# A gated mix of full and windowed attention: first key weights by ACT's queue, last keys and last norm in halves, a third slice for GpSimd, and a new order

## The chip, the core and the metric

The kernel runs on one core of a Trainium2 chip. The metric is the device time of one execution in microseconds. Before the change it is 780.96 us, the median of three runs (780.86 to 782.89). The traces come from one profiled execution each. Engines go by the names of the profile: PE (TensorE, matmuls), PEld (its weight loads), DVE (VectorE), ACT (ScalarE), POOL (GpSimd) and SP (which issues most transfers). L12 is line 12 of the kernel.

## The reference

The input x is one sequence of 2048 tokens and 640 features in bf16. Two attentions with 32 heads of 20 features are computed from it, one over all keys, one over a dilated window of 8 keys, and their outputs are mixed by a gate.

```
B, S, D = 1, 2048, 640
g = sigmoid((x * gate_w).sum(-1, keepdims=True))
# A: full attention
q, k, v = split_heads(x @ A_wqkv)              # 32 heads of 20
p = softmax(q @ k.T * 20 ** -0.5)
a = merge_heads(p @ v) @ A_wo
# B: token s sees s, s-2, ..., s-14, with weights of its own
b = merge_heads(softmax_over_8(q . k[s - 2 w]) . v[s - 2 w]) @ B_wo
out = g * a + (1 - g) * b
```

## The kernel before, in words

**Units and tiles.** The scores of A are computed as keys by queries. Work is cut into groups (512 queries, four heads; 32 groups) and, within a group, into units of one head, 128 keys and 512 queries: 64 per group, 2048 in all. A tile is two or three units: PE writes their scores into PSUM (L1941, `qk`), and ACT takes the exponential of a whole tile into `ebuf` (L1959, `exp`). The sums over keys, weighted by v, go to one PSUM bank, `obank` (L2004, `pv`). Four heads stand on top of each other, so four units go through PE side by side.

**Units without ACT.** Some units take another way. DVE shifts and clamps the raw score into a 16-bit integer (`clamp`, L1918, tile `uD`), which read as bf16 is a coarse exponential. Three copies of it, each with another constant added (`SHIFTS`), are made as tile `eD`, and PE adds the four slices, weighted by constants in copies of v (`vS`, L1087 on POOL), in `obank`. Such units are taken in quads: the four heads of one block of keys. In the text a slice is one of these copies, k = 1, 2, 3. `gen_d` (L1037) makes what is left of a slice with one DVE instruction of 512, 1024, 1536 or 2048 columns. `piece` lets POOL make one unit of a slice ahead of it (L1068); it looks at the slices in `KPIECE`, (1, 2) before. `eD` has room for three slices, and a slice's room is free when the one three before it has gone through PE.

**The order.** The file holds its own scheduler: `_Sched.task` books each operation on an engine with an assumed duration and derives the semaphores from the buffers that it reads and writes. Generators (`gen_b` and `gen_bproj` for attention B, `gen_norm`, `gen_fold`, `gen_v`, `gen_q1` and others) offer side work, which is put between the tiles. When an operation is taken, and whether a tile carries a quad's unit, hangs on some twenty constants (`SLACK`, `DWAIT`, `DIDLE`, `PTAPS`, ...). `PLAN` replaces them at given tile numbers: 126 sets before. All of this runs when the program is built; on the chip each engine has a fixed list, which it works off in order. POOL's operations are booked into windows beside DVE instructions of at least 0.59 us that don't use the port that DVE and POOL share, as the code has it (`slot`). `PTAPS` says how many products of attention B are made by POOL (L1196, L1304).

**The start.** SP loads x in eight pieces of 256 tokens (`x_load`, L553), the key weights of the first four heads behind the first piece (L558), and later the query weights (L561) and the rest. POOL pads the weights (L653). PE transposes x piece by piece (`turn`, L1633), ACT and DVE copy the result to `xT` (L1643, L1647), and PE computes the keys of the first four heads in four blocks of 512 (`k_first`, L1653). For each block DVE finds the largest absolute key (`k_max`, L1670), and ACT copies the block to `kT` (`k_out`, L1677). From the maxima and the absolute queries (ACT L1730, DVE L1731) comes a bound per query that is subtracted from the scores: L1712, L1714, L1728, then a matmul (L1735). The order of the start is a string, `HEAD`, with a letter for the operation and a digit for the block.

**The end.** The last group's sums are normalized by `gen_norm_last`: transpose, reciprocal, gate, scale and transpose back, each over all 512 queries. `tail` adds the last four heads to the projected output. The earlier heads are added before that, in `gen_prefold`, `gen_prefold2` and the first part of `tail`. The last fold runs through the right strips of four blocks of 128 tokens (128 columns each), then the left 512 columns of blocks 2, 3, 0 and 1. DVE adds the strips to what was computed before (L1458), ACT copies blocks 2 and 3 (L1464), DVE adds blocks 0 and 1 (L1467), and four transfers write them out (L1472).

**The output weights of B.** `constants` loads them (L644, tile `woBp`), in four transfers, each when SP's queue is quiet.

Of the kernel before, what the change touches and what calls it, by code (L numbers as in the profile page):

```python
# [5 lines left out]
FP32 = mybir.dt.float32  # L6
# [46 lines left out]
    0: ((0.326, 0.478), 0.0, 1, 1.0, 0.79, -1.09, -0.25, 10.72, 2.0, 9.17, 0.45, 0.36, 3.46, 3.61, 0.0, 0.59, 1, -2.32, 0.3, -1.0, (2, 2)),  # L53
    5: ((0.318, 0.419), 0.0, 1, 1.0, 0.79, -1.09, -0.25, 4.03, 2.0, 9.17, 0.45, 0.52, 3.46, 3.61, 0.0, 0.59, 1, -2.32, 0.3, -1.0, (2, 2)),
    10: ((0.326, 0.478), 0.16, 1, 1.79, 0.79, -1.26, -0.25, 11.51, 3.71, 8.58, 0.4, 0.67, 3.16, 3.61, -0.23, 0.59, 1, -5.33, 0.3, -1.0, (0, 2)),
    15: ((0.34, 0.55), 0.16, 1.0, 1, 0.75, -1.26, -0.13, 7.8, 4.71, 6.0, 0.91, 0.2, 6.33, 4.29, 0.03, 0.59, 1, -5.33, 0.3, -1.0, (2, 2)),
    20: ((0.34, 0.55), 0.25, 6.6, 1.0, 1.09, -1.26, -0.13, 7.8, 6.7, 7.19, 0.85, 0.32, 3.46, 4.29, 0.0, 0.71, 1, -3, 0.3, -1.0, (2, 0)),
    25: ((0.373, 0.716), 0.27, 6.6, 1.0, 1.21, -1.26, -0.13, 11.42, 6.7, 7.19, 0.85, 0.32, 3.46, 4.29, 0.0, 0.71, 1, -3, 0.3, -1.0, (2, 0)),
    30: ((0.343, 0.845), 0.31, 6.6, 1.0, 1.21, -1.26, -0.25, 11.42, 6.7, 7.19, 0.85, 0.32, 3.46, 4.29, 0.0, 0.71, 1, -3, 0.3, -1.0, (0, 2)),
    35: ((0.34, 0.55), 0.16, 1.0, 1, 0.69, -1.26, -0.43, 7.8, 4.71, 6.0, 0.91, 0.49, 5.31, 4.29, -0.03, 0.59, 1, -5.33, 0.3, -1.0, (2, 0)),  # L60
    40: ((0.326, 0.478), 0.16, 1, 1.79, 0.79, -1.26, -0.25, 11.51, 3.71, 8.58, 0.4, 0.67, 3.16, 3.61, -0.03, 0.59, 1, -5.33, 0.3, -1.0, (0, 2)),
    45: ((0.326, 0.478), 0.16, 1, 4.63, 0.79, -1.26, -0.25, 11.51, 3.71, 8.58, 0.4, 0.67, 3.16, 3.61, 0.12, 0.59, 1, -5.33, 0.3, -1.0, (1, 2)),
    50: ((0.34, 0.51), 0.25, 1, 1.0, 0.89, -1.26, -0.43, 7.8, 8, 5.03, 0.91, 0.32, 5.31, 3.77, 0.08, 0.59, 2, -6, 0.3, -1.0, (2, 2)),
    55: ((0.34, 0.51), 0.33, 1, 1.0, 0.89, -1.26, -0.24, 11.51, 8, 9.17, 0.65, 0.32, 5.31, 4.74, 0.08, 0.59, 2, -6.71, 0.3, -1.0, (2, 2)),
    60: ((0.353, 0.546), 0.33, 1, 1.0, 0.89, -1.26, -0.24, 11.51, 8, 9.17, 0.65, 0.32, 5.31, 4.74, 0.08, 0.59, 2, -6.71, 0.3, -1.0, (2, 2)),
    65: ((0.34, 0.51), 0.39, 1, 1.0, 0.89, -1.26, -0.43, 7.8, 7.0, 9.43, 0.91, 0.32, 5.31, 4.07, 0.08, 0.59, 2, -6, 0.3, -1.0, (2, 2)),
    70: ((0.34, 0.51), 0.4, 1, 1.0, 0.89, -1.26, -0.43, 7.8, 7.0, 9.43, 0.91, 0.3, 5.31, 4.07, 0.08, 0.59, 2, -6, 0.3, -1.0, (2, 2)),
    75: ((0.34, 0.51), 0.4, 1, 1.0, 0.89, -1.26, -0.94, 7.8, 7.0, 9.43, 0.91, 0.3, 5.31, 4.07, 0.08, 0.59, 2, -6, 0.3, -1.0, (2, 2)),
    85: ((0.34, 0.51), 0.4, 1, 1.0, 0.75, -1.26, -0.94, 7.8, 7.0, 9.43, 0.91, 0.3, 5.31, 3.41, 0.08, 0.59, 2, -6, 0.3, -1.0, (2, 2)),
    90: ((0.34, 0.51), 0.4, 1, 1.0, 0.75, -1.26, -0.34, 7.8, 7.0, 9.43, 0.83, 0.3, 5.31, 3.41, 0.08, 0.59, 2, -6, 0.3, -1.0, (2, 0)),  # L70
    95: ((0.389, 0.582), 0.4, 1, 1.0, 0.96, -1.26, -0.34, 7.8, 7.0, 9.43, 0.83, 0.39, 5.31, 3.41, 0.08, 0.69, 2, -6, 0.3, -1.0, (2, 0)),
    100: ((0.389, 0.582), 0.4, 1.13, 1.0, 0.96, -1.26, -0.34, 7.8, 7.0, 7.05, 0.98, 0.39, 5.31, 3.41, 0.08, 0.69, 2, -6, 0.3, -1.0, (1, 0)),
    105: ((0.389, 0.582), 0.4, 1.13, 1.0, 0.96, -1.26, -0.34, 7.8, 7.0, 7.05, 0.98, 0.65, 5.31, 3.25, 0.08, 0.69, 2, -6, 0.3, -1.0, (1, 0)),
    110: ((0.34, 0.51), 0.25, 1.13, 1.0, 0.96, -1.26, -0.43, 7.8, 1, 5.03, 0.98, 0.61, 5.31, 2.74, 0.08, 0.69, 2, -6, 0.3, -1.0, (2, 2)),
    120: ((0.278, 0.663), 0.39, 1.0, 1.0, 1.17, -1.6, -1.28, 2, 1, 4.68, 0.56, 0.57, 4.56, 4.29, -0.03, 0.65, 2, -5.46, 0.3, -1.0, (2, 2)),
    125: ((0.291, 0.715), 0.39, 1.0, 1.0, 0.94, -1.6, -0.92, 2, 2.0, 4.68, 0.64, 0.57, 4.56, 4.29, 0.0, 0.68, 2, -3, 0.3, -1.0, (2, 2)),
    130: ((0.291, 0.715), 0.39, 1.0, 1.0, 0.94, -1.48, -0.92, 2, 1, 4.68, 0.64, 0.57, 4.56, 4.29, -0.05, 0.68, 2, -3, 0.3, -1.0, (2, 2)),
    135: ((0.291, 0.715), 0.39, 1.0, 1.0, 0.94, -1.48, -0.92, 2, 1, 4.68, 0.64, 0.57, 4.56, 4.29, -0.11, 0.68, 2, -3, 0.3, -1.0, (2, 2)),
    140: ((0.291, 0.715), 0.39, 1.0, 1.0, 0.94, -1.48, -0.92, 7.8, 1, 4.68, 0.64, 0.32, 4.56, 4.29, 0.0, 0.68, 2, -3, 0.3, -1.0, (2, 2)),
    145: ((0.241, 0.719), 0.39, 1.0, 1.0, 0.94, -1.48, -0.92, 7.8, 1, 4.68, 0.64, 0.32, 4.56, 4.29, 0.0, 0.68, 2, -3, 0.3, -1.0, (2, 2)),  # L80
    150: ((0.241, 0.719), 0.39, 1.0, 1.0, 0.79, -1.48, -0.92, 7.8, 1, 4.68, 0.64, 0.32, 4.56, 4.29, 0.0, 0.73, 2, -1.5, 0.3, -1.0, (2, 2)),
    155: ((0.241, 0.719), 0.41, 1.61, 1.0, 0.79, -1.48, -0.92, 9.65, 1, 4.68, 0.69, 0.32, 4.56, 4.29, 0.0, 0.73, 2, -1.5, 0.3, -1.0, (2, 2)),
    160: ((0.241, 0.719), 0.41, 1.61, 1.0, 0.79, -1.48, -0.92, 9.65, 8, 4.68, 0.69, 0.32, 4.56, 4.7, 0.0, 0.73, 2, -1.5, 0.3, -1.0, (2, 2)),
    165: ((0.241, 0.719), 0.41, 1.61, 1.0, 0.79, -1.48, -0.92, 9.65, 1, 4.89, 0.69, 0.32, 4.56, 4.7, 0.0, 0.73, 2, -1.5, 0.3, -1.0, (2, 2)),
    170: ((0.207, 0.746), 0.41, 1, 1.0, 0.79, -1.48, -0.92, 9.65, 1, 5.2, 0.69, 0.32, 4.56, 4.7, 0.0, 0.73, 2, -1.5, 0.3, -1.0, (2, 2)),
    175: ((0.207, 0.746), 0.41, 1, 1.0, 0.79, -1.75, -0.92, 9.33, 1, 5.2, 0.69, 0.32, 4.56, 4.7, 0.0, 0.73, 2, -1.5, 0.3, -1.0, (1, 0)),
    180: ((0.207, 0.746), 0.41, 1, 1.0, 0.79, -1.75, -0.92, 9.33, 1, 5.2, 0.69, 0.32, 4.56, 4.7, 0.08, 0.73, 2, -1.5, 0.3, -1.0, (1, 0)),
    185: ((0.421, 0.553), 0.41, 1, 1.0, 0.79, -1.75, -0.34, 7.8, 1, 6.0, 0.69, 0.32, 6.33, 4.7, 0.08, 0.59, 2, -1.5, 0.3, -1.0, (1, 0)),
    190: ((0.421, 0.553), 0.41, 1, 1.0, 0.79, -1.75, -0.43, 7.8, 1, 7.54, 0.96, 0.32, 6.33, 4.7, 0.08, 0.59, 2, -1.5, 0.3, -1.0, (0, 2)),
    195: ((0.421, 0.553), 0.41, 1, 1.0, 0.79, -1.75, -0.43, 4.47, 1, 7.54, 0.96, 0.32, 6.33, 4.8, 0.08, 0.59, 2, -1.5, 0.21, -1.0, (0, 2)),  # L90
    200: ((0.421, 0.553), 0.33, 1, 1.0, 0.75, -1.75, -0.43, 4.47, 1, 7.54, 0.96, 0.32, 6.33, 4.8, -0.1, 0.59, 2, -1.5, 0.21, -1.0, (0, 2)),
# [327 lines left out]
def _build(ctx, nc, A_x, A_wqkv, A_wo, B_wqkv, B_wo, gate_w, out):  # L419
# [185 lines left out]
    def constants():  # L605
# [35 lines left out]
        for j in range(4):  # L641
            while not quiet():
                yield ("cond",)
# [1594 lines left out]
```

## Time and profile before

The profiled execution took 780.83 us; its span, from the first to the last instruction, is 779.0 us, and 1.83 us lie around it. The granted TensorE clock is 1.000.

| stage | us of the span | what is busy |
|---|---|---|
| start, to the first exponential | 0 to 18.52 | transfers and warm-up matmuls, then PE, ACT and DVE in turn |
| body, exponentials | 18.52 to 769.78 | ACT 745.19 of 751.30 with the exponentials alone |
| end | 769.78 to 779.0 | norm on DVE, folds on PE, transfers out |

| operation | count | mean ns | busy us |
|---|---|---|---|
| exponential, ACT L1959 | 710 | 1197 | 745.2 |
| clamp, DVE L1918 | 428 | 681 | 287.2 |
| slices, DVE L1037, all shapes | 287 | 620 | 171.7 |
| slice pieces, POOL L1068 | 288 | 617 | 173.6 |
| weighted v, POOL L1087 | 107 | 615 | 65.9 |
| filler matmuls, PE L2025 | 324 | 379 (median) | 27.6 |

How to read such lines: a group has its line, engine and operation, the tile written and the tiles read, the shapes and the count; behind the first bar the busy time in us and the mean ns of one; behind the second the idle time of the engine just before these instructions, and what ended most of it. Mean times of instructions that overlap on their engine add up to more than the busy time. A chain has the start in us, the length in us, and what it was.

### The profile page before, as it was taken

The page shows a single profiled execution, that of the slowest core. Times are in us where ns is not written, and L with a number is a line of the kernel's source. Part 1 is how long each engine was busy: PE and PEld are TensorE (multiplying, and loading weights), DVE is VectorE, ACT ScalarE, POOL GpSimd, SP SyncE. Part 2 cuts the span into 40 slices and gives each one's busy share as a digit, 9 for nine tenths or more (in the row PEclk, how much of TensorE's full clock was granted, in tenths as well). Part 3 has the DMA queues.
Part 4 walks back from the last instruction along what each step waited for, and adds up shares of the span by engine and source line. Part 5 has one row for each costly group of instructions (what it writes and reads, how often), then busy time and mean ns, then how long its engine had stood idle before and what let it go on. Part 6 is the DMA issues. An engine that isn't in the chain of part 4 may idle for free.

```text
span 779.0 us, 30108 instructions
## 1 busy us (share of the span) xinstructions
PE 747.8 (96%) x12412; PEld 288.3 (37%) x12412; DVE 695.2 (89%) x1245; ACT 758.2 (97%) x749; POOL 333.8 (43%) x570
## 2 busy tenths in 40 slices
PE   8999999999999999999999999999999999999987
PEld 5433333232343433433344324333444433343223
DVE  6688898999899999998899999988999998799995
ACT  5999999999999999999999999999999999999995
POOL 4133553445543543333355344624444553333531
PEclk9999999999999999999999999999999999999999
DMA  7321212011121423311123233024112421320311
GB/s 230 114 62 39 52 43 61 24 42 24 44 66 45 98 55 96 93 48 35 48 70 84 57 81 94 20 52 102 45 30 60 106 53 49 89 55 22 91 44 40
DMA packets 71456, 49.89 MB, mean 64 GB/s; under 512 B 43096, under 2 KB 64872, under 8 KB 71320
## 3 DMA queue, kind: packets, MB, share of 16 engines
q1 hardware_dynamic: 71032, 47.64, 24.3%
q8 instruction: 99, 1.62, 0.9%
q14 instruction: 37, 0.30, 0.1%
q10 hardware_dynamic: 288, 0.33, 0.1%
HBM read 32.79 MB, written 7.62 MB: 52 GB/s over the span
## 4 chain that ended last, share of the span: by engine, by line
PE 49%; ACT 27%; issue 11%; DVE 11%; DMA 2%; SPq 0%; POOL 0%; DVEq 0%; ACTq 0%
ACT ebuf L1959 27%; PE score L1941 15%; PE obank L2004 14%; PE side L687 12%; PE score L687 4%; DVE uD L1918 3%; DVE eD L1037 2%; DVE kvw L1314 1%; DVE qkvB L1143 1%; DVE kvw L1205 1%; DMA woBp<-in_B_wo_dram 1%; PE side L1218 1%; DMA oTd<-in_A_x_dram 1%; PE side L1326 1%; DMA scr_q<-qbnd 0%
## 5 line engine op out<-in xcount | busy, mean ns | idle before, releaser
L1959 ACT ACTIVATE ebuf<-score 128x1024 bf16<-128x1024 f32 (+1 forms) x710 | 745.2, 1197 | 3.1 <-PE score L1941 2.0
L1918 DVE TENSOR_SCALAR uD<-score 128x512 int16<-128x512 f32 x428 | 287.2, 681 | 34.5 <-PE score L1941 32.1
L1941 PE MATMUL score<-qT,kT 32*128 32x512 bf16 x1856 | 259.0, 384 | 12.7 <-ACT ebuf L1959 9.2
L1068 POOL TENSOR_TENSOR eD<-uD,two 128x256 int32<-128x256 int32 x288 | 173.6, 617 | 116.8 <-DVE eD L1037 53.7
L1037 DVE TENSOR_SCALAR eD<-uD 128x2048 int16<-128x2048 int16 (+3 forms) x287 | 171.7, 620 | 5.7 <-PE obank L2004 5.0
L2004 PE MATMUL obank<-ebuf,vA 128*21 128x512 bf16 x1620 | 153.3, 385 | 0.3
L1941 PEld LDWEIGHTS score<-qT,kT 32*128 32x128 bf16 x1856 | 64.0, 91 | 210.4 <-ACT ebuf L1959 149.8
L1087 POOL TENSOR_TENSOR vS<-vA,vw 128x252 bf16<-128x252 bf16 x107 | 65.9, 615 | 117.2 <-DVE eD L1037 63.5
L2004 PE MATMUL obank<-eD,vS 128*21 128x512 bf16 x1284 | 110.8, 380 | 0.4 <-POOL eD L1068 0.3
L687 PE MATMUL side<-xT,wBs 128*32 128x256 bf16 x2400 | 97.4, 281 | 2.9 <-DVE qkvB L1143 1.4
L687 PEld LDWEIGHTS side<-xT,wBs 128*32 128x32 bf16 x2400 | 68.4, 141 | 33.9 <-issue 15.4
L1010 POOL TENSOR_TENSOR oN<-oTt,oN 128x256 bf16<-128x256 f32 x60 | 44.8, 746 | 74.3 <-DVE eD L1037 37.8
L2004 PEld LDWEIGHTS obank<-ebuf,vA 128*21 128x21 bf16 x1620 | 36.8, 89 | 83.6 <-issue 62.4
L995 POOL TENSOR_TENSOR rcp<-rcp,gA 128x16 f32<-128x16 f32 x30 | 7.6, 252 | 95.6 <-DVE eD L1037 63.6
L1143 DVE CAST qkvB<-side 128x512 bf16<-128x512 f32 (+1 forms) x72 | 42.1, 594 | 4.5 <-PE side L687 4.2
L1205 DVE TENSOR_TENSOR kvw<-qkvB 128x2048 bf16<-128x2048 bf16 (+2 forms) x40 | 45.0, 1146 | 0.6 <-PE side L1218 0.5
L1314 DVE TENSOR_TENSOR kvw<-kvw,eB 128x2048 bf16<-128x2048 bf16 (+1 forms) x40 | 45.5, 1157 | 0.0
L2004 PE MATMUL obank<-uD,vA 128*21 128x512 bf16 x428 | 41.5, 379 | 0.0
L2004 PEld LDWEIGHTS obank<-eD,vS 128*21 128x21 bf16 x1284 | 30.8, 91 | 20.2 <-DVE eD L1037 2.3
L687 PE MATMUL side<-xT,kvw 128*32 128x512 bf16 (+1 forms) x360 | 30.4, 383 | 0.8 <-DVE vA L913 0.2
L1941 PE MATMUL score<-woBp,kT 32*128 32x512 bf16 x192 | 30.0, 384 | 0.5
L687 PE MATMUL side<-kvw,xT 128*32 128x160 bf16 (+1 forms) x700 | 27.4, 265 | 1.3 <-DVE small L749 0.6
(195 smaller groups left out, 566.6 us busy)
## 6 DMA issues: line engine op xcount, KB each, us to landing
kvw<-scr_v SPq DMA_DIRECT2D x32, 336.5 KB
oN<-scr_n SPq DMA_DIRECT2D x60, 128.0 KB
scr_v<-qkvB SPq DMA_DIRECT2D x32, 85.0 KB
wBs<-in_B_wqkv_dram SPq DMA_DIRECT2D x5, 480.0 KB
WqP<-in_A_wqkv_dram SPq DMA_DIRECT2D x14, 160.0 KB
oTd<-oN SPq DMA_DIRECT2D x108, 20.0 KB
out_dram<-outsb SPq DMA_DIRECT2D x12, 160.0 KB
qT<-dst SPq DMA_DIRECT2D x93, 20.0 KB
```

The costliest lines, as they stand in the source:

```text
L687: ins = e.matmul(o[j:k, :], l(j) if callable(l) else l[:, j:k], r, start=(first and i == 0), stop=(last and i == n - 1), skip_group_check= ...
L1010: T("pool", 0.73, lambda e, cols=cols: e.tensor_tensor(oN[0][:, cols], oTt[:, cols], rcpR[:, cols], ALU.mult), reads=["oTt", "oN%d" % i], ...
L1037: T("dve", 0.065 + 0.1334 * (n - m), lambda e, k=k, sl=sl, m=m: e.tensor_scalar(eD[:, sl % NS, 512 * m:512 * n].bitcast(I16), uD[d % 2][:, ...
L1068: T("pool", PDUR, lambda e: e.tensor_tensor(eD[:, sl % NS, 512 * i:512 * (i + 1)].bitcast(I32), uD[d % 2][:, 512 * i:512 * (i + 1)].bitcas ...
L1087: T("pool", 0.607, lambda e: e.tensor_tensor(vS[:, d % 2, :, :], _ap(vA, (kb * NQ + q) * 4 * DV, [[0, K - 1], [1, 4 * DV]]), _ap(vw, 0, [[ ...
L1143: t = TB(dvc(n * TOK), lambda e, o=o, i=i: e.tensor_copy(o, i), reads=[("side", b)], writes=[key])
L1205: TB(dvc(n_ * TOK, 2), lambda e: e.tensor_tensor(o, i0, i1, ALU.mult), reads=["qB", "kB"], writes=prods(i, range(n_)) + olds(), port=True)
L1314: TB(dvc(n_ * 2 * TOK, 2), lambda e: e.tensor_tensor(o, i0, i1, ALU.mult), reads=rd, writes=prods(i, range(2 * n_)), port=True)
L1918: t = T("dve", 0.598, lambda e: e.tensor_scalar(uD[d % 2][:, 512 * i:512 * (i + 1)].bitcast(I16), side[x], UOFF, 0.0, op0=ALU.add, op1=ALU ...
L1941: ins = e.matmul(o, kT[32 * j:32 * j + 32, q, kb * P:(kb + 1) * P], qT[qbuf[g]][32 * j:32 * j + 32, :], start=True, stop=True)
L1959: exps[s] = T("act", actc(512 * n), lambda e: e.activation(ebuf[s % NE][:, 0:512 * n], score[s % 2][:, 0:512 * n], ACTF.Exp, scale=LN2 / S ...
L2004: ins = e.matmul(obank[32 * j:32 * j + DV, :], v, src, start=(kb == 0), stop=(last and k >= len(lst) - 4), skip_group_check=True)
```

## The change

1. The transfer of the first key weights is issued by ACT's queue instead of SP's, and the eight pieces of x follow each other on SP. The query weights stay on SP.
2. The keys of the first heads are computed in five blocks instead of four: three of 512 and two of 256. Block 2 goes to PSUM bank 2 instead of bank 0, block 3 to bank 0, block 4 to `obank`. The maximum is taken and the block copied for each of the five. The second half of the absolute queries is made by ACT instead of DVE.
3. The last norm is made in halves of 256 queries, second half first, and the last fold goes half by half: strips of blocks 2 and 3, their left columns, strips of blocks 0 and 1, their left columns.
4. `KPIECE` is (1, 2, 3): POOL may make pieces of the third slice too. `PLATE`, how late a piece may start, becomes a constant of the plan (0.13 to 0.28).
5. `woBp` may be loaded when the scheduler is past group 12, quiet or not.
6. `PLAN` has 121 sets of 22 values in place of 126 sets of 21. Only 4 of the tile numbers that occur in either keep the values that held there.
7. Some assumed durations and issue times of the scheduler differ.

The diff without the plan, cut to its core:

```diff
-    x_load(0, 4.1)
-    T("sp", 4.6, lambda e: e.dma_start(w4(ebuf[3]), wA_v[:, :, D:D + 4 * DH]), writes=[("ebuf", 3)], dma=True, iss=0.5)
-    for p, t in enumerate((5.4, 6.6, 7.4, 8.3, 9.2, 10.1, 11.0)):
-        x_load(p + 1, t - 0.78 - 0.28 * p)
+    T("act", 5.0, lambda e: e.dma_start(w4(ebuf[3]), wA_v[:, :, D:D + 4 * DH]), writes=[("ebuf", 3)], dma=True, iss=0.45)
+    for p, t in enumerate((4.0, 5.6, 6.5, 7.4, 8.3, 9.2, 10.1, 11.1)):
+        x_load(p, t - 0.28 * p)
...
-        while not done.get(("norm", 8)) or g1 <= QLAST or not done.get(("qs", 1, 2)) or not calm():
+        while not done.get(("norm", 8)) or g1 <= QLAST or not done.get(("qs", 1, 2)) or not (calm() or cur["g"] > 12):
...
-            while not quiet():
+            while not (quiet() or cur["g"] > 12):
...
-        T("dve", 0.625, lambda e: e.transpose(oTt[:, :], obank[:, :]), reads=["obank"], writes=["oTt"])
...
+        for op, h in ((turn_o, 1), (turn_o, 0), (inv, 1), (inv, 0), (gate_r, 1), (gate_r, 0), (scale_o, 1), (scale_o, 0), (back, 1), (back, 0)):
+            op(h)
...
-    KPIECE = (1, 2)
+    KPIECE = (1, 2, 3)
...
-        mm(("score", 1), [fold_mms(strip(blk), blk, q, 512, D, False)[0] for blk in range(4)], True)
-        for blk in (2, 3):
-            b = tail_bank[blk]
-            mm(("side", b), fold_mms(side[b][:, :], blk, q, 0, 512, False), True)
-        for blk in range(2):
-            mm(("score", 0), fold_mms(half(blk), blk, q, 0, 512, False), True)
+        for h in (1, 0):
+            mm(("score", 1), [fold_mms(strip(blk), blk, q, 512, D, False)[0] for blk in (2 * h, 2 * h + 1)], True, rd[h])
+            for blk in (2 * h, 2 * h + 1):
+                if h:
+                    b = tail_bank[blk]
+                    mm(("side", b), fold_mms(side[b][:, :], blk, q, 0, 512, False), True, rd[h])
+                else:
+                    mm(("score", 0), fold_mms(half(blk), blk, q, 0, 512, False), True, rd[h])
...
-    kbank = lambda tcc: ((side[0], ("side", 0)), (side[1], ("side", 1)), (side[0], ("side", 0)), (obank, "obank"))[tcc]
+    kbank = lambda i: ((side[0], ("side", 0)), (side[1], ("side", 1)), (side[2], ("side", 2)), (side[0], ("side", 0)), (obank, "obank"))[i]
+    kcol = lambda i: ((0, 512), (512, 512), (1024, 512), (1536, 256), (1792, 256))[i]
...
-    HEAD = ("t0 w0 w1 x0 t1 x1 y0 y1 a0 t2 b0 x2 y2 m0 t3 x3 o0 t4 y3 x4 y4 t5 k1 y5 x5 t6 x6 m1 t7 x7 y6 k2 o1 "
-            "y7 k3 m2 o2 q0 c0 m3")
+    HEAD = ("t0 x0 w0 w1 t1 x1 y0 y1 a0 t2 b0 x2 y2 m0 t3 x3 o0 t4 y3 x4 y4 t5 k1 y5 x5 t6 x6 m1 t7 x7 y6 k2 o1 "
+            "y7 k3 m2 k4 o2 m3 q0 c0 o3 m4")
...
-    T("dve", dvc(256), lambda e: e.tensor_scalar(
-        qabs[0][:, 256:512].bitcast(U16), side[2].bitcast(U16)[:, 1:512:2], 0x7FFF, None, op0=ALU.bitwise_and),
-      reads=[QB[1]], writes=[("qabs", 0)])
+    T("act", actc(256), lambda e: e.activation(qabs[0][:, 256:512], qb[1], ACTF.Abs), reads=[QB[1]], writes=[("qabs", 0)])
...
-             FILL, HOLD, BOFF, EVS, FRT, PTAPS) = plan
+             FILL, HOLD, BOFF, EVS, FRT, PTAPS, PLATE) = plan
```

The letters of `HEAD`: t transposes a piece, x and y copy it (ACT, DVE), a and b are the halves of the first key block, k is a key block, m its maximum, o its copy to `kT`, q the first queries, c the maximum over the earlier blocks, w a warm-up matmul.

## The prediction

> **What bounds the kernel now.** I read the page's busy shares first, then a table of busy time over the stretch in which the exponentials run, then the groups of instructions with their shapes, and last the chains at both ends, because a bound read from the whole span mixes three stages.
>
> ```profile
> PE 747.8 (96%) x12412; PEld 288.3 (37%) x12412; DVE 695.2 (89%) x1245; ACT 758.2 (97%) x749; POOL 333.8 (43%) x570
> L1959 ACT ACTIVATE ebuf<-score 128x1024 bf16<-128x1024 f32 (+1 forms) x710 | 745.2, 1197 | 3.1 <-PE score L1941 2.0
> ```
>
> These are two lines of the page. ScalarE's 710 exponentials fill 745.2 us and were kept waiting 3.1 us in all. The first starts at 18.52 us and the last ends at 769.78, by the timeline. The table by stretches, 20 to 770 us, closes with this sum:
>
> ```profile
> sum 750.00, PE 726.18 PEld 274.98 DVE 678.58 ACT 746.35 POOL 324.15; mean PE 90.77 PEld 34.37 DVE 84.82 ACT 93.29 POOL 40.52
> ```
>
> Of 750.00 us ACT is busy 746.35, so 3.65 are idle, while DVE idles 71.4 and GpSimd 425.9. PE looks nearly as full, but 324 of its matmuls, 81 groups of four, are fillers (L2025) that give way to real work. So the body, 751.3 us, is ACT's: it gets shorter only when units of work leave ACT. A unit is one head's 128 keys by 512 queries. There are 2048; DVE takes the 428 of L1918, ACT 1620, which is 745.2/1620 = 0.460 us each. DVE takes units four at a time, a "quad" (107 of them). One quad more takes 4 x 0.460 = 1.84 us from the body.
>
> What a quad costs DVE, and what GpSimd takes of that, stands in the groups by shape:
>
> ```profile
> L1918 DVE TENSOR_SCALAR uD<-score 128x512 int16<-128x512 f32 x428 | 287.2, 681 | 34.5 <-PE score L1941 32.1
> L1068 POOL TENSOR_TENSOR eD<-uD,two 128x256 int32<-128x256 int32 x288 | 173.6, 617 | 116.8 <-DVE eD L1037 53.7 <-DVE kvw L1314 18.3 <-DVE uD L1918 16.7
> L1037 DVE TENSOR_SCALAR eD<-uD 128x2048 int16<-128x2048 int16 x203 | 137.1, 692 | 5.5 <-PE obank L2004 5.0
> ...
> L1037 DVE TENSOR_SCALAR eD<-uD 128x512 int16<-128x512 int16 x20 | 5.8, 291 | 0.1
> ```
>
> A quad is four clamps of 0.681 and three shifted slices of 0.692, 4.80 us. A slice of one unit takes 0.291, of four 0.692, so one unit less saves (0.692 - 0.291)/3 = 0.134 us, and the last one 0.291. GpSimd now makes 288 pieces of one unit, of the first two slices only.
>
> The start is not ACT's. Its chain begins so:
>
> ```profile
> 0.74 0.46 SPq L553
> 1.20 0.06 issue
> 1.25 0.46 SPq L558
> 1.71 0.04 issue
> 1.75 5.01 DMA oTd<-in_A_x_dram
> 6.76 0.05 issue
> ```
>
> SP issues input piece 0, then the key weights (L558), then piece 1, whose data are there at 6.76; PE has nothing but warm-ups until then. The end is PE's. Its last pieces:
>
> ```profile
> 770.44 2.16 PE score L687 x40
> 772.60 1.53 PE score L1436 x64
> 774.13 0.22 PE side L1436 x4
> 774.35 0.68 PE score L1436 x12
> 775.03 0.02 issue
> 775.05 0.69 DVE kvw L1467
> ```
>
> PE folds without a break from the last attention matmul (770.23) to 775.03. The last norm, on DVE, runs from 770.28 to 772.76 beside it (the timeline's L943 to L952), and PE asks for it only at about 773.5. It has 0.75 us of room.
>
> **The change part by part**, against the profiled execution: 780.83 us, of which 779.0 are the span and 1.83 lie around it. The median of three is 780.96, 0.13 above.
>
> **Start, key weights by ACT's queue.** SP loses one issue, 0.50 us (1.25 to 1.75), ahead of piece 1 and the six after it. On ACT the issue comes before its table load (1.28) and warm exponential; nothing on ACT is needed until 5.08, and the warm one ends at 2.24, so 0.46 is hidden; without that cover it would cost its 0.46. GpSimd waits for these weights (L653 at 4.22); their product is asked for at 7.33, with 2.6 us of room for 0.52 of copy. Best case: the dip in DMA traffic closes too (84 to 161 GB/s between 3.5 and 5 us, over 300 after), about 1.0 us in all. Worst case: from 5 to 16 us the DMA engines are full (364 to 394 GB/s at their best), piece 5 still lands at 10.47, where PE waits 0.37 today, and the gain is 0. I take 0.5, the issue itself, nearest to a row. The Trainium skill (Trainium Kernel Development and Optimization, "Key Constraints"; DMA: Bandwidth & Descriptors, "Issuing engines are not separate DMA queues") says that DMAs from several engines run on the same 16 DMA engines and that only issue time is saved; by it the gain is these 0.5, and the 1.0 is ruled out. The trace of before has one queue here, so it can't show it.
>
> **Start, last 512 keys in halves, bound of the first queries on ACT.** One product of 1.24 us becomes two halves on PE, the same columns. On DVE the chain from 14.56 to 16.72 (maximum 0.70, small ones 0.17 and 0.29, maximum 0.68, L1728 0.35) becomes 0.70 + 0.41 + 0.46 + 0.41 + 0.35 = 2.33 instead of 2.16 (0.41: a 256-column row, L1143's 413 ns). That is 0.2 later. In exchange the 0.42 of L1731, now behind it, goes to ACT, whose copies (0.68, and half that) leave it free at about 16.8; its two absolutes of 0.38 end near 17.1, where L1731 ended at 17.15. New wait: the second query product takes bank 2, which the third key block now holds until ACT has copied it (about 16.0); PE reaches it at 16.2. Between -0.1 and +0.2; I take 0.
>
> **Body, GpSimd on the third slice and a new order.** Pieces run beside DVE's 512-column reads. The groups list 428 + 48 + 30 + 20 + 20 + 20 + 16 + 12 + 8 + 5 = 607 of these, and GpSimd work placed in them is 288 + 107 + 60 + 30 + 24 + 22 = 531. So 76 windows at most are open, worth 76 x 0.134 = 10.2 us of DVE, which pays for two quads (9.6). With DVE's own 71.4 idle us the ceiling is far higher, (71.4 + 10.2)/4.80 = 17 quads, -31 us; the floor is that no piece more is made, 0, or that a different order is worse, below. I take **two quads, -3.7**, since the windows are the resource that the change opens and the idle time was there before. PE gets three groups more per quad, 20 matmuls being 1.21 us: 6 x 0.24 = 1.5, in place of fillers. Which tile rides when is decided by 121 sets of constants, nearly all changed; I can't read their sum from a trace.
>
> **Body, weights of the second projection.** woBp may be loaded without waiting for a quiet queue. Today PE waits 0.72 for them at 344.37 and ACT then 0.21. At most 0.2 gained; against it a norm's transfer may queue behind issues of up to 1.6 us on SP. 0.
>
> **End, the norm in halves and the folds in halves.** Ten DVE steps in place of five take some 2.3 to 2.9 us instead of 2.48, inside 0.75 us of room: 0. But the right strips, made first in one run of 0.22, now come half before and half after two folds of 0.22. The strip addition (L1458, 0.69) waits for both halves, starts 0.44 later, and the two additions behind it on DVE (L1467) end the kernel; today the first starts at 775.05, then at 774.63 + 0.69 = 775.32: **+0.3**. If more of the folding is done before 770, the halved norm becomes the end and up to 0.9 is won; bounds -0.9 to +0.3.
>
> **Sum:** 780.83 - 0.5 - 3.7 + 0.3 = 776.9; with the 0.13 of the median, **777.1 us**.
>
> **The rivals.** (A) *No quad more*: the windows are open because nothing was ready then, and third-slice pieces only take the place of others. For it: 531 of 607 are used; DVE waits 32.1 us for PE at L1918, so it lacks scores, not time. Against: a third candidate per quad widens what fits. 780.96 - 0.5 + 0.3 = 780.8.
>
> (B) *The order gives more*: four quads. For it: 71.4 idle us on DVE, 81 filler groups on PE. 780.96 - 0.5 - 7.4 + 0.3 = 773.4.
>
> (C) *The third slice comes late, slower*. GpSimd's pieces wait for DVE:
>
> ```profile
> POOL eD L1068 <- DVE eD L1037: 53.7, 42, 4.6
> ```
>
> This is a line of the table of waits: us in total, times, longest. 42 of 288 pieces waited 1.28 us on average for a DVE shift. Of the first two slices that is hidden (PE waited for L1068 some 0.8 us in all), but the third is the last that a quad's matmuls need, and PE issues in order, so its wait reaches the scores and ACT has 3.65 us of slack in all. 76 pieces at 42/288 are 11 late ones, 14.2 us; with half of it behind the exponential under way (1.0 to 1.4 us) 7.1: 777.1 + 7.1 = 784.2 with the quads, 787.9 without. I put 785. It decides once PE's waits for L1068 pass some 4 us. The Trainium skill (SBUF — State Buffer, "Who interferes with whom") calls the port pair that DVE's fast modes and GpSimd share an exclusive lock, held for the whole instruction; by that rule each piece on the wrong side of a shift waits for all of it. The trace agrees in kind: the waits above, and 3 of 1284 slice loads and matmuls that then waited for a piece.
>
> **How the numbers follow.** Forecast (one to three quads) 0.46, A 0.22, B 0.14, C 0.18. No measurement of this kernel tells less than 0.3% from no change, that is 778.6 to 783.3. Forecast and B lie below: faster 0.60; A within: 0.22; C above: 0.18. The range takes in the forecast, A, most of B (six quads: 769.7) and C up to its price: 770.5 to 785.0, which leaves out some 0.13.
>
> **What would show it.** Piece 1 landing near 6.2 and the first exponential near 18.0 (0.0 or 1.0 earlier marks my bounds); L1918 at 436 instead of 428, ACT units 1612; GpSimd pieces above 288, up to 364, and DVE shifts of four units fewer per quad; PE's waits for pieces under 2 us; the strip addition about 0.4 later after PE's last fold begins. It would be wrong if ACT's idle time in the body grows beyond some 4 us, if L1918 stays at 428, or if DVE's windows fill and quads don't follow.

## The result, and the profile after

The kernel after takes 778.51 us (median of 6 runs, 777.98 to 778.74), the kernel before 781.39 (6 runs beside it, 780.86 to 782.89). The ratio is 0.996, 95% interval 0.9947 to 0.9973: faster by 0.4%. The profiled execution took 778.55 us, 2.28 less than the one of before. By the timeline's first and last exponential:

| stage | before | after | difference |
|---|---|---|---|
| start, to the first exponential | 18.52 | 17.29 | -1.23 |
| body, first to last exponential | 751.26 | 750.25 | -1.01 |
| end, to the end of the span | 9.22 | 9.16 | -0.06 |
| around the span | 1.83 | 1.85 | +0.02 |

Line numbers moved: the exponential is now L1973, the scores L1955, the clamp L1932, DVE's slices L1048, POOL's pieces L1079, the attention sums L2018, the fillers L2039, the transposes of the start L1646, the last folds L1447, the strip addition L1471.

**The body.** Two lines of the page after, busy shares and exponentials, and the sum of the table by stretches, here from 20.0 to 767.5 us:

```profile
PE 749.7 (97%) x12484; PEld 290.9 (37%) x12484; DVE 697.6 (90%) x1270; ACT 756.5 (97%) x751; POOL 359.0 (46%) x616
...
L1973 ACT ACTIVATE ebuf<-score 128x1024 bf16<-128x1024 f32 (+1 forms) x710 | 742.9, 1198 | 5.1 <-PE score L1955 3.6
```

```profile
sum 747.50, PE 726.90 PEld 276.19 DVE 680.58 ACT 742.89 POOL 349.31; mean PE 726.90 PEld 276.19 DVE 680.58 ACT 742.89 POOL 349.31
```

The exponentials are busy 2.3 us less (745.2 before), which is five units of 0.460. But they are kept waiting 2.0 us more (5.1 against 3.1), most of it for PE's scores. With 0.7 us that ACT no longer waits at L933 (below, woBp) this is the body's -1.0. The units show in the groups by shape:

```profile
L1932 DVE TENSOR_SCALAR uD<-score 128x512 int16<-128x512 f32 x433 | 291.3, 684 | 33.8 <-PE score L1955 31.6
...
L1079 POOL TENSOR_TENSOR eD<-uD,two 128x256 int32<-128x256 int32 x331 | 198.2, 613 | 136.0 <-DVE eD L1048 61.6 <-DVE uD L1932 17.3 <-DVE kvw L1325 17.3
...
L1048 DVE TENSOR_SCALAR eD<-uD 128x2048 int16<-128x2048 int16 x169 | 115.6, 704 | 2.8 <-PE obank L2018 2.3
...
L1048 DVE TENSOR_SCALAR eD<-uD 128x512 int16<-128x512 int16 x36 | 10.6, 297 | 0.1
```

Clamps went from 428 to 433: 108 quads and one unit more, not 109 quads. POOL makes 331 pieces instead of 288, and DVE has 169 full slices of four units instead of 203, in all 1.5 us more of slices (173.2 against 171.7). Counted by slice in the two programs, the pieces are 196 of the first, 92 of the second and none of the third before, and 170, 73 and 88 after: 45 of the 88 took the place of others.

**The start.** The chain of waits after begins with SP's issues of x, one behind the other. Its next lines, up to the transposes of piece 5:

```profile
3.25 0.04 issue
3.29 5.91 DMA oB<-in_A_x_dram
9.20 0.09 issue
9.29 0.72 PE score L1646 x10
```

Piece 1 (before: in the chain at 6.76) is no longer in it; now it is piece 5, there at 9.20. The table by stretches gives 191 GB/s of DMA traffic from 0 to 5 us, where it gave 121 before; from 4 to 5 us alone it is 385 and 123.

**The end**, by the chain from the last attention matmul on:

```profile
768.20 1.73 PE score L681 x32
769.93 1.42 PE score L1447 x56
771.35 0.22 PE side L1447 x4
771.57 0.36 PE score L1447 x12
771.92 0.02 issue
771.95 0.69 DVE kvw L1471
```

PE folds for 3.7 us after its last attention matmul (768.20 to 771.92), before for 4.8 (770.23 to 775.03).

### The profile page after: what moved, and what is told of

Same layout as the page of the kernel before. It is cut to its first block, busy times and chain, and to the rows that moved or that the text cites. A ratio compares the mean times of both kernels' runs of the same rounds, so it can differ in the third digit from the quotient of the medians.

```text
span 776.7 us, 30340 instructions
## 1 busy us (share of the span) xinstructions
PE 749.7 (97%) x12484; PEld 290.9 (37%) x12484; DVE 697.6 (90%) x1270; ACT 756.5 (97%) x751; POOL 359.0 (46%) x616
## 4 chain that ended last, share of the span: by engine, by line
PE 49%; ACT 30%; issue 13%; DVE 6%; DMA 1%; SPq 0%; ACTq 0%; DVEq 0%
ACT ebuf L1973 30%; PE score L1955 16%; PE obank L2018 14%; PE side L681 12%; PE score L681 4%; DVE uD L1932 2%; DVE eD L1048 1%; DMA oB<-in_A_x_dram 1%; PE side L1337 1%; PE side L1229 1%; PE score L2039 1%; DVE kvw L1216 0%; PE score L1666 0%; PE obank L2039 0%; DVE dst L831 0%
## 5 line engine op out<-in xcount | busy, mean ns | idle before, releaser
L1973 ACT ACTIVATE ebuf<-score 128x1024 bf16<-128x1024 f32 (+1 forms) x710 | 742.9, 1198 | 5.1 <-PE score L1955 3.6
L1932 DVE TENSOR_SCALAR uD<-score 128x512 int16<-128x512 f32 x433 | 291.3, 684 | 33.8 <-PE score L1955 31.6
L1955 PE MATMUL score<-qT,kT 32*128 32x512 bf16 x1856 | 258.8, 384 | 12.6 <-ACT ebuf L1973 9.3
L1079 POOL TENSOR_TENSOR eD<-uD,two 128x256 int32<-128x256 int32 x331 | 198.2, 613 | 136.0 <-DVE eD L1048 61.6
L1048 DVE TENSOR_SCALAR eD<-uD 128x2048 int16<-128x2048 int16 (+3 forms) x302 | 173.2, 596 | 3.1 <-PE obank L2018 2.3
L2018 PE MATMUL obank<-ebuf,vA 128*21 128x512 bf16 x1615 | 152.8, 385 | 1.3 <-ACT ebuf L1973 1.1
L1955 PEld LDWEIGHTS score<-qT,kT 32*128 32x128 bf16 x1856 | 63.8, 91 | 209.0 <-ACT ebuf L1973 148.1
L2018 PE MATMUL obank<-eD,vS 128*21 128x512 bf16 x1299 | 113.1, 379 | 0.0
L681 PEld LDWEIGHTS side<-xT,wBs 128*32 128x32 bf16 x2400 | 67.4, 142 | 34.1 <-issue 16.8
L2018 PEld LDWEIGHTS obank<-ebuf,vA 128*21 128x21 bf16 x1615 | 37.0, 89 | 82.9 <-issue 56.7
L2018 PE MATMUL obank<-uD,vA 128*21 128x512 bf16 x433 | 42.3, 379 | 0.0
L2018 PEld LDWEIGHTS obank<-eD,vS 128*21 128x21 bf16 x1299 | 31.8, 91 | 20.0 <-issue 2.5
L1955 PE MATMUL score<-woBp,kT 32*128 32x512 bf16 x192 | 29.5, 384 | 1.8 <-ACT ebuf L1973 1.8
L1207 POOL TENSOR_TENSOR kvw<-qkvB 128x256 bf16<-128x256 bf16 x29 | 17.5, 614 | 26.9 <-DVE kvw L1216 11.4
```

Of the source, the lines that this page charges most:

```text
L681: ins = e.matmul(o[j:k, :], l(j) if callable(l) else l[:, j:k], r, start=(first and i == 0), stop=(last and i == n - 1), skip_group_check= ...
L1048: T("dve", 0.065 + 0.1334 * (n - m), lambda e, k=k, sl=sl, m=m: e.tensor_scalar(eD[:, sl % NS, 512 * m:512 * n].bitcast(I16), uD[d % 2][:, ...
L1079: T("pool", PDUR, lambda e: e.tensor_tensor(eD[:, sl % NS, 512 * i:512 * (i + 1)].bitcast(I32), uD[d % 2][:, 512 * i:512 * (i + 1)].bitcas ...
L1932: t = T("dve", 0.598, lambda e: e.tensor_scalar(uD[d % 2][:, 512 * i:512 * (i + 1)].bitcast(I16), side[x], UOFF, 0.0, op0=ALU.add, op1=ALU ...
L1955: ins = e.matmul(o, kT[32 * j:32 * j + 32, q, kb * P:(kb + 1) * P], qT[qbuf[g]][32 * j:32 * j + 32, :], start=True, stop=True)
L1973: exps[s] = T("act", actc(512 * n), lambda e: e.activation(ebuf[s % NE][:, 0:512 * n], score[s % 2][:, 0:512 * n], ACTF.Exp, scale=LN2 / S ...
```

## The experiments

**Theory.** Start: the key weights, 640 runs of 160 bytes, hold up piece 1 on their queue by more than their issue. Rival: only the issue counts. Body: PE, in an order fixed when the program is built, bounds it together with ACT. Rival: ACT alone. Third slice: it pays, or it only displaces. Each kernel has one profile; the intervals are those of whole runs. Body means from the first exponential's start to the last one's end.

Identical lists do not give identical times: in six profiles whose lists for the body are those of after (after, e2, e7, e8, e12, e13) the body takes 749.43 to 750.36, mean 749.98; with the lists of before (before, e1, e3) 751.26, 751.97, 751.39, mean 751.54. So the body gained 1.0 in the profiled pair and 1.6 by these means.

**e1, the kernel before with change 1 alone.** Just before the program is written out:

```diff
+    wk = sch.lists["sp"].pop(1)
+    wk.stream = "act"
+    sch.lists["act"].insert(0, wk)
     sch.emit()
```

> Before, with one edit made after all scheduling: the transfer of the first key weights leaves SP's list and stands first in ACT's; every other list is that of before. In before the second group of transposes started at 6.81 us and the first exponential at 18.52. Theory 1 (on one queue the 640 short runs of 160 bytes of the key weights hold up the piece of x behind them): the second transposes start by 5.4, the first exponential at 17.3 to 17.5, and the total falls by 1.0 to 1.3 us. Rival 2 (only SP's issue time is saved, as the prediction had it): 6.3, 18.0 and 0.5 us. Rival 3 (the new start gains by its halved keys and the absolutes on ACT, not by the queue): no more than rival 2 here.

First exponential 17.47, 1.05 earlier; 779.98 us (10 runs) against 781.04 (14), ratio 0.9984 [0.9974, 0.9994]. The second ten transposes in PE's timeline of before, then the same stretch in e1:

```profile
6.81 0.73 PE L1633 MATMUL score<-ident,oTd 128*128 128x128 bf16 x10 [1.33 <-DMA oTd<-in_A_x_dram]
```

```profile
4.18 1.27 PE L1633 MATMUL score<-ident,oTd 128*128 128x128 bf16 x10
5.25 0.68 PE L583 MATMUL obank<-qabs 128*128 128x512 bf16 x2
5.77 0.72 PE L1633 MATMUL score<-ident,oTd 128*128 128x128 bf16 x10
```

The second ten transposes follow the warm-ups (L583) without a wait for data, which was 1.33 us before. Change 1 alone brings the start's gain; in whole runs it is 1.06 us by the medians, 0.5 to 2.0 by the interval.

**e2, the kernel after with change 1 undone:** the weights go back to second place in SP's list.

```diff
+    wk = sch.lists["act"].pop(0)
+    wk.stream = "sp"
+    sch.lists["sp"].insert(1, wk)
     sch.emit()
```

> After, with the reverse edit: the key weights' transfer goes back behind the first piece of x on SP, all else as in after, where the second transposes start at 5.22 and the first exponential at 17.29. Theory 1: 6.7 to 6.9 and 18.4 to 18.6, total 1.0 to 1.3 us above after (779.5 to 779.8). Rival 2: 5.7 and 17.8, 0.5 us. Rival 3: 17.3 to 17.8, since the halves and the absolutes on ACT stay.

First exponential 18.24, 0.95 later than after; 779.32 us (5 runs), ratio 0.9967 [0.9954, 0.9981], 0.8 above after. PE waits again, by its timeline:

```profile
6.09 0.73 PE L1646 MATMUL score<-ident,oTd 128*128 128x128 bf16 x10 [0.61 <-DMA oTd<-in_A_x_dram]
```

The direction is as expected, the size less: 6.7 to 6.9 and 18.4 to 18.6 were expected. With the same issue times on the same queue, piece 1 is here 0.7 earlier than in before; by that much single profiles can differ. Piece 5 is a second measure: PE waits for its data until 10.25 in e2, and until 9.29, 9.39 and 9.66 in after, e13 and e4. The pieces come 0.6 to 1.0 earlier without the weights on their queue, and one issue is 0.50. Change 2 may be some 0.2 to 0.3 quicker by itself (18.24 against 18.52; 17.47 in e1 to 17.29), which is no more than such spreads.

**e3, the kernel before with the weights in long runs.** The same bytes on the same queue as 128 runs of 800 bytes instead of 640 of 160; what arrives are not the key weights, so the kernel computes with other keys.

```diff
-dma_start(w4(ebuf[3]), wA_v[:, :, D:D + 4 * DH])
+dma_start(_ap(ebuf[3], 0, [[1, 20 * DH]]), A_wqkv[0:P, D:D + 20 * DH])
```

> Before, with the key weights' transfer still on SP behind the first piece of x, but reading 128 runs of 800 bytes instead of 640 of 160, the same 102 KB: it leaves out the right key weights of the first four heads (it loads other columns). If the number of short runs is what holds up the next piece: the second transposes start at 5.3 to 6.0 instead of 6.81, the first exponential at 17.3 to 17.9. If any transfer ahead on the queue costs the same: 6.7 to 6.9 and 18.4 to 18.6.

```profile
5.93 0.73 PE L1633 MATMUL score<-ident,oTd 128*128 128x128 bf16 x10 [0.19 <-DMA oTd<-in_A_x_dram]
```

Second transposes at 5.93 (6.81 before), first exponential 18.00, one run 780.44. By this pair alone short runs would cost 0.52 (18.52 to 18.00). But e2 has the short runs too, and there the second transposes begin at 6.09, 0.16 later than here. Two profiles with the short runs lie further apart (6.81 and 6.09) than e2 and e3, so it is not shown that the run length matters. What does go with the queue is a dip in traffic: from 4 to 5 us the table by stretches gives 123, 189 and 205 GB/s in before, e2 and e3, and 274 to 385 in all eleven profiles with the weights on ACT's queue. Why the dip comes stays open.

**e6, two slices only.** The kernel after, with its plan kept; the order is then planned anew.

```diff
-    KPIECE = (1, 2, 3)
+    KPIECE = (1, 2)
```

> After, built with pieces of the first two slices only, and its own plan. The scheduler then books 97 quads instead of 109 and 255 pieces instead of 331, and ACT has 1660 units instead of 1615. Theory A (a plan fits one program; changed behind its back it loses far more than the slice is worth): at least the 45 units x 0.460 = 20.7 us above after, with waits 30 to 70. Rival B (the plan is robust, the third slice alone carries the gain): 2 to 6 us above after.

844.17 us (one run, at a granted clock of 0.989). The exponentials' line on its page:

```profile
L1973 ACT ACTIVATE ebuf<-score 128x1024 bf16<-128x1024 f32 (+1 forms) x726 | 767.2, 1190 | 34.1 <-PE score L1955 32.2
```

388 clamps, 255 pieces, 34.1 us of waits at the exponentials, as theory A had it. The constants fit one program; with a rule changed under them they say nothing of what the rule is worth. That is what e4 is for.

**e4, the third slice back on DVE, all orders kept.** 68 of the 88 third-slice pieces are dropped from POOL's list, and the DVE instruction of their slice does their units as well (d3 holds it with its quad d, the units n that it had left and its place; gone are the dropped pieces):

```diff
+    for d, ps_ in p3.items():
+        if d in d3:
+            t, n, sl = d3[d]
+            t.fn = lambda e, d=d, n=n, sl=sl: e.tensor_scalar(
+                eD[:, sl % NS, 0:512 * n].bitcast(I16), uD[d % 2][:, 0:512 * n].bitcast(I16), SHIFTS[3], None, op0=ALU.add)
...
+    sch.lists["pool"] = [t for t in sch.lists["pool"] if id(t) not in gone]
     sch.emit()
```

> After, with the order of every list kept, but 68 of the 88 pieces of the third slice taken off GpSimd and made by the DVE instruction that makes the rest of that slice (the 20 pieces of slices that GpSimd makes alone stay). GpSimd pieces 263 instead of 331; DVE gets 68 x 0.134 = 9.1 us more work. Theory A (the new order lives on the time that the third slice frees on DVE): DVE comes late, its slices reach PE late, and the total rises by 3 to 9 us above after (778.5). Rival B (DVE idles 67 us in the body, the pieces matter only for what the scheduler dared to book): less than 1 us.

POOL keeps 263 pieces, DVE is busy 703.1 us instead of 697.6, and the exponentials wait no longer than in after (5.3 against 5.1). Body 751.08, 1.1 above the mean of after; 780.17 us (10 runs), ratio 0.9984 [0.9969, 0.9998], 1.7 above after's median and 1.9 by the ratios (0.9984 - 0.996, of 781). The interval overlaps that of after, but against e8 and e9, timed beside it, it is 1.6 and 1.5 by the medians of ten runs each. Neither theory's number: the 68 pieces save DVE 5.5 us, and a fifth to a third of that reaches the end. That is as much as the whole body gained, 1.0 to 1.6.

**e9, ten exponentials one unit shorter.** Ten of ACT's 1615 units are left out; their rows keep old values.

```diff
-ebuf[s % NE][:, 0:512 * n], score[s % 2][:, 0:512 * n], ACTF.Exp
+ebuf[s % NE][:, 0:512 * (n - (s % 70 == 35))], score[s % 2][:, 0:512 * (n - (s % 70 == 35))], ACTF.Exp
```

> After, with ten exponentials, one in seventy, one unit of 512 columns shorter: it leaves out ten of the 1615 units that ACT makes, all other instructions stay. If the body is ACT's: 10 x 0.41 to 0.46 = 4.1 to 4.6 us below after. If PE, 97% busy, is a second bound and its fixed order holds the next scores: 0 to 2 us.

```profile
L1973 ACT ACTIVATE ebuf<-score 128x1024 bf16<-128x1024 f32 (+1 forms) x710 | 740.0, 1183 | 7.7 <-PE score L1955 6.2
```

This line of its page decides (ten units at 0.460 would have been 4.6): busy time fell by 2.9 (742.9 to 740.0) and waiting rose by 2.6 (5.1 to 7.7), all of it for PE. Body 749.98, the same as with all units; 778.65 us (10 runs), ratio 0.9963 [0.9952, 0.9973]. ACT work that is taken away comes back as waiting, so the body is not ACT's alone.

**e10, no fillers.** The 94 groups of filler matmuls (376) are dropped from PE's list and the waits that they carried are passed to PE's next operation.

```diff
+    for t in sch.lists["pe"]:
+        if id(t) in ids:
+            prev[id(t)] = last
+            owed += t.deps
+        else:
+            t.deps = t.deps + owed
+            owed, last = [], t
+            kept.append(t)
...
+    sch.lists["pe"] = kept
     sch.emit()
```

> The kernel after without its 94 groups of filler matmuls (376, some 27 us of PE); everything else keeps its place, and the lists of the other engines are the same. Nothing of the result depends on them. Theory A: the waits of the exponentials for PE (3.6 us) come from what PE's list holds between two tiles, and fillers are part of that, because a filler in a fixed list gives way to nothing. Without them the exponentials' idle time falls from 5.1 to 3 us or less, the body from a mean of 750.0 to about 748, and the time to about 776.5. Theory B: the fillers stand only where PE has time left, so they hide nothing and cost nothing: idle time 5 us, 778.5. Theory C: they keep TensorE's clock up: the granted clock falls below 0.99 and the time rises above 780.

The profiled run, at a granted clock of 0.999, took 777.89, with a body of 748.87:

```profile
PE 731.2 (94%) x12107; PEld 284.2 (37%) x12108; DVE 696.1 (90%) x1270; ACT 755.6 (97%) x751; POOL 357.6 (46%) x616
...
L1973 ACT ACTIVATE ebuf<-score 128x1024 bf16<-128x1024 f32 (+1 forms) x710 | 742.2, 1207 | 4.5 <-PE score L1955 3.1
```

Without the fillers PE is busy 18.5 us less (749.7 to 731.2), fewer than the 27 that were expected. By this profile 1.1 us of body are gained at that clock, about half of what theory A wanted. But 9 of the 12 runs had a granted clock of 0.990 to 0.994 and took 780.06 to 781.46; the three at 0.997 to 0.999 took 777.89 to 778.65. The median is 780.92 (before beside it: 781.14, 28 runs; ratio 0.999 [0.9978, 1.0001]). Theory C holds in these nine runs, with a clock just above the 0.99 that it named: fillers cost perhaps one us in PE's list, by the one profile, and save some 2.4, the difference to after's median (2.65 to e12's, timed beside it).

**e11, no fillers, and ten short exponentials:** the edits of e9 and e10 together.

> The kernel without fillers, with the ten exponentials one unit shorter (ten of ACT's 1615 units are left out, 2.9 us of ACT). With fillers this gained nothing: ACT's idle time took all of it. Theory A (the fillers are what PE is late with): now the body shortens by 2 to 3 us against the kernel without fillers, some 774. Theory B (PE's real work in its fixed places, and DVE's clamps, set the times of the tiles): again within 0.5 us of the kernel without fillers.

780.51 us (12 runs), ratio 0.9996 [0.9982, 1.001]. Run by run at the same clock: 777.10 against 777.89 at 0.999, and a mean of 780.5 (5 runs) against 781.1 (6 runs) at 0.992. So 2.9 us of ACT work are worth 0.6 to 0.8 here at most; the runs of the two overlap, and the medians differ by 0.4. Without the fillers, with PE less busy, ACT's work still hardly counts; so the sum of PE's work does not look like the bound either. What is left is theory B, the fixed places of PE's real work or DVE's clamps; no run parts these two. The profiled run (780.8 us span, clock 0.991) shows how the clock goes. Table by stretches; behind the five engines stands the granted clock:

```profile
742.00:744.00 2.00, 0.94 (x17) 0.33 (x17) 1.94 (x2) 2.00 (x3) 0.00 (x0) 1.00 0.08 21
744.00:746.00 2.00, 1.11 (x18) 0.38 (x22) 1.23 (x3) 2.00 (x3) 1.18 (x2) 1.00 0.08 21
746.00:748.00 2.00, 1.66 (x22) 0.37 (x22) 2.00 (x4) 2.00 (x3) 0.73 (x2) 0.91 0.00 0
748.00:750.00 2.00, 2.00 (x34) 0.82 (x31) 1.50 (x3) 1.65 (x2) 2.00 (x4) 0.50 0.00 0
750.00:752.00 2.00, 2.00 (x58) 1.32 (x59) 1.69 (x5) 1.36 (x2) 0.16 (x1) 0.73 0.03 8
752.00:754.00 2.00, 2.00 (x82) 1.22 (x78) 1.45 (x4) 2.00 (x2) 1.55 (x3) 1.00 0.00 0
```

PE is busy only half the time from 742 to 746 (0.94 and 1.11 of 2 us); from 747.7 to 751.1, worked out from the clock in these rows, the clock is halved, PE is full, and ACT, busy throughout until then, loses 0.35 and 0.64 us. Another stretch lies at 761.3 to 764.7, and one of twice the length at 252.7 to 259.6.

**e7 and e8, the end taken apart.** e7 is after with `gen_norm_last` and the last folds of before (the lines marked - for them in the change's diff, in place of those marked +); e8 keeps the halved norm but makes all four strips first:

```diff
         for h in (1, 0):
             mm(("score", 1), [... for blk in (2 * h, 2 * h + 1)], True, rd[h])
+        for h in (1, 0):
             for blk in (2 * h, 2 * h + 1):
```

> After, with the last norm whole and the folds in the order of before (all four strips first). The stage from the end of the last attention matmul to the end of the last addition on DVE is 768.20 to 773.83 = 5.63 us in after, 770.23 to 776.34 = 6.11 in before. By the prediction's step (PE's folds set the end, the strips' addition comes late when the folds go half by half, the halved norm gains nothing): 0.2 to 0.4 shorter than after, 5.25 to 5.45. By the rival (the halved norm is what PE waits for, since after has less folding left after the last attention matmul): no shorter, 5.6 to 5.9.

> After, with the halved norm kept but the right strips of all four blocks folded first (second half's pair, then first half's pair), then the left columns. By the prediction's step: the strips' addition starts 0.3 to 0.4 us sooner after the last folds begin, and the end comes 0.2 to 0.4 us sooner than in after (stage from the last attention matmul to the last addition 5.25 to 5.45 instead of 5.63). By the rival (the first half's norm isn't ready for its strips): PE waits for it and the stage is 5.6 or more.

From the end of the last attention matmul to the end of the last addition it takes 5.63 us in after (768.20 to 773.83), 5.47 in e7 (767.56 to 773.03) and 5.47 in e8 (767.85 to 773.32). Halving the norm is worth nothing; the order of the folds costs 0.16, less than the 0.2 to 0.4 expected. In whole runs: 777.59 for e7 (one run) and 778.53 for e8 (10 runs, ratio 0.9955 [0.994, 0.997]), which is not to be told from after.

**e12, strips first, and the key weights behind ACT's table load and warm exponential.** In e8:

```diff
+    wk = sch.lists["act"].pop(0)
+    sch.lists["act"].insert(1, wk)
     sch.emit()
```

> The kernel after with all four strips first and with ACT issuing the key weights behind its table load and warm exponential (near 2.3 us) instead of first (0.74). Theory 1, the short runs of this transfer hold up whatever competes with it: piece 1 lands earlier still, second transposes at 5.0 or before, first exponential 17.0 to 17.2, and 777.9 to 778.3 in all. Rival: the padding on GpSimd, which waits for these weights, becomes late (from 4.37 to some 6) and the first products of keys wait for it: first exponential 17.3 or later, 778.5 or above.

ACT issued the weights at 0.91, not 2.3: the engine's table load (0.74 to 2.02) did not hold the transfer up. So the edit tested little; 778.27 us (11 runs), ratio 0.9966 [0.9957, 0.9976]. Yet its first exponential came at 18.14, and PE's timeline shows why, beside e8's, whose came at 17.28. First e12, then e8:

```profile
4.18 1.27 PE L1647 MATMUL score<-ident,oTd 128*128 128x128 bf16 x10
5.25 1.06 PE L577 MATMUL obank<-qabs 128*128 128x512 bf16 x2
6.10 1.06 PE L1647 MATMUL score<-ident,oTd 128*128 128x128 bf16 x10
```

```profile
4.03 0.72 PE L1647 MATMUL score<-ident,oTd 128*128 128x128 bf16 x10
4.58 0.59 PE L577 MATMUL obank<-qabs 128*128 128x512 bf16 x2
5.08 0.73 PE L1647 MATMUL score<-ident,oTd 128*128 128x128 bf16 x10
```

The same instructions take up to 1.8 times as long until PE reaches its full early rate: near 4 us in e8, near 6.8 in e12. Over after and its variants with this start, the first exponential lies between 17.28 and 18.22 for this reason. At its late end (18.03 to 18.22 in e9 to e12) it comes no earlier than in e2, which has the weights on SP's queue and a quick PE (18.24). So the 1.05 and 0.95 of e1 and e2 hold for the moment at which PE became quick in those profiles.

**e13, strips first, without the two warm-ups between the transposes of pieces 0 and 1.** The edit of e10, with `w0` and `w1` of `HEAD` in place of the fillers:

```diff
-"w": lambda i: T("pe", 0.2, warm_up, reads=[("qabs", 0)], writes=["obank"])}
+"w": lambda i: fills.append(T("pe", 0.2, warm_up, reads=[("qabs", 0)], writes=["obank"]))}
```

> The kernel after with all four strips first and without the two warm-up matmuls that stand between the transposes of pieces 0 and 1 (nothing of the result depends on them). In the profiles of after and of its variants PE no longer waits for piece 1; it runs those two in 0.59 to 1.06 us, and the ten transposes of a piece in 0.72 us at its full early rate and in 1.27 before it. Theory P (with the data earlier, PE itself is late next): the second transposes begin at 5.0 to 5.5 in the timeline even where PE is still slow, the first exponential comes at 17.2 to 17.6, and the time falls by 0.3 to 0.6, to 777.8 to 778.2. Rival D (pieces 4 and 5, for which PE waits at 8.3 and 9.3 in the quickest of the starts, set the end of the start): first exponential 17.3 or later and 778.5 as with the warm-ups. Rival W (PE reaches its full rate only after so much work, and the two matmuls are part of it): the transposes of pieces 1 and 2 take over 1 us each and the first exponential comes at 18 or later.

PE was slow until about 6.2 here (twenty transposes in 2.05 us), and still the first exponential came at 17.39, as P has it. But PE then waits at 9.39 for piece 5, as D has it, and the time is 778.42 us (6 runs, ratio 0.996 [0.9948, 0.9972]), not to be told from e8's. So in this one profile a late start of PE's full rate cost little once the warm-ups were out of its way.

No version was faster than after by more than the runs can tell; e7, e8, e12 and e13 lie within 777.6 to 778.6.

## Why the prediction was right, and where it was not

The sign and the place of the two gains were right, the time 1.4 too low. Term by term: body 2.7 too much, start 0.7 and end 0.4 too little. That the sum came so near is partly luck: what start and end brought beyond the forecast covered 1.1 of the 2.7 that the body lacked.

**Start: "I take 0.5, the issue itself".** Mis-sized: 1.05 by e1, 0.95 by e2, near the prediction's own best case of 1.0, in which the dip in traffic closes too, and the dip did close (385 instead of 123 GB/s from 4 to 5 us). What the move saves beyond the issue was put down to the 640 short runs, which e2 and e3 together do not show. The Trainium skill (DMA: Bandwidth & Descriptors, "Issuing engines are not separate DMA queues") leaves only the issue time; the profiles here differ, with pieces 0.6 to 1.0 earlier. The same page ("Specifications") puts the size below which a transfer loses line rate at 512 bytes; e3's step from 160 to 800 crosses it, and its 0.16 to e2 doesn't tell whether that counts here. PE also had more to do before piece 1 than "nothing but warm-ups": the ten transposes of piece 0 (4.18). The feared worst case, piece 5 landing no earlier than 10.47, did not come: it was there at 9.20. What the prediction did not ask is what is late next. It is PE itself, slow in its first microseconds, which the wait of 1.33 us for piece 1 had covered. The Trainium skill (TensorE: Matmul & The Clock Gate, "Part 1: The HAM clock gate") says that PE starts at half rate until some 3.4 us of activity have been seen by a window that is not tied to the kernel's start; the rows above agree in kind, 2.8 to 5.6 us after the first matmul at 1.22. The granted clock reads 1.00 all the while.

**Halves and absolutes, 0:** 0.2 to 0.3 gained (e1 to after; before to e2), near the bound of 0.1 and smaller than the spread that PE's slow start makes. Not settled.

**Body: "two quads, -3.7"** is the step that failed. Five units came, not eight, of which 2.0 us were given back as waits. Two reasons failed. "76 windows are open" counted those that POOL could use: 43 more pieces were made, and half of the third slice's (45 of 88) displaced others, as rival A had it. And "the body is ACT's", since fillers "give way to real work": in a fixed list nothing gives way, there are 94 groups now and not 81, and e9 shows that 2.9 us less on ACT are worth nothing: ACT then waits for PE's scores. Nor is it PE's 726 of 750 us as a sum, for with 18.5 of them gone the body is only 1.1 shorter (e10) and ACT's work still hardly counts (e11). The fixed lists let no tile come earlier; whether PE's matmuls between two tiles or DVE's clamps hold it is open. So rival A was half right, and its time (780.8) and the forecast's (777.1) lie on both sides of the result.

**Rival C** did not come. The table of waits of after, beside the 53.7 us in 42 times of before:

```profile
POOL eD L1079 <- DVE eD L1048: 61.6, 73, 1.9
```

More pieces wait for a DVE shift, but 0.84 us on average instead of 1.28. PE's own waits for pieces rose from 0.8 us (0.5 at weight loads, 0.3 at matmuls) to 1.8, all at weight loads and none longer than 0.4; that is under the 2 us which the prediction named, and under the 4 from which this case decides. What 68 of the 88 third-slice pieces bring, with every order kept (e4), is 1.1 to 1.9 us; what the new order brings without them was not tried.

**woBp, 0:** PE's wait of 0.7 us for these weights (at its weight loads; 0.42 at the matmuls) is gone from its table, and so are 0.7 us that ACT waited at L933 for a norm. They are part of the body's difference; what each is worth was not tried.

**End: "+0.3".** Halving the norm 0, as predicted (e7 and e8 agree to 0.01). The strip order costs 0.16 instead of 0.3. That fits the additions on DVE, which start 0.60 apart (771.95, 772.55, 773.15 by the timeline), where the prediction took 0.69. Less folding was left behind the last attention matmul (3.7 us of it instead of 4.8), and that saved more than the order cost: from there to the last addition it is 6.11 before and 5.63 after. It does not reach the end of the span: the last attention matmul comes 0.2 later behind the last exponential (0.65 instead of 0.45), and from the last addition to the end it is 2.87 instead of 2.66.

## What to carry to other kernels

Where engines hand each other tiles in fixed lists, an engine that is 97% busy need not be the bound alone. Shorten a few of its instructions and see whether its waits grow by the same amount, before counting on work taken from it. When a wait goes, ask what ran slowly beneath it. A transfer ahead of others on one queue can cost them more than its issue; look at the traffic behind it. And before a difference of half a microsecond between two single profiles is given a cause, look for two profiles of the same thing.

## What the runs showed of the hardware

- Without the 376 filler matmuls the granted clock was 0.990 to 0.994 in 9 of 12 runs. With ten exponentials shortened as well (e11) the profiled run shows it in stretches of about 3.4 us, or twice that, at 0.50; the one shown follows 4 us in which PE was half idle. In e10 a mean clock lower by 0.007 went with some 3.2 us (777.89 at 0.999; a mean of 781.1 of six runs at 0.992).
- PE's first matmuls are slower than later ones (ten transposes take 1.27 or 0.72 us), and the moment at which this ends varied from near 4 (e8) to near 7 us (e9 to e12) with the same start of PE's list. The granted clock reads 1.00 all the while.
- With 0.1 MB of key weights behind piece 0 on SP's queue the traffic from 4 to 5 us was 123 to 205 GB/s in three profiles; with them on ACT's queue it was 274 to 385 in eleven.
- A DMA issue placed behind ACT's table load in its list went out at 0.91 us (e12), while the load ran from 0.74 to 2.02.
